# Block 0's outputs take later places in VectorE's order (eleven empty slots for six, pauses of one slot for two), and wo for block 0 is loaded from SyncE's queue

## The chip, the cores and the metric

The kernel runs on one core of one Trainium2 chip. Five engines work on their own instruction streams and meet through semaphores: TensorE (PE in the profile, with its weight loads as PEld), VectorE (DVE), ScalarE (ACT), GpSimd (POOL) and SyncE (SP), which here only starts DMAs. The metric is the device time of one execution in microseconds, taken as the median of several runs.

## The reference

One transformer block on 2048 tokens of width 512: layer norm, attention with 32 query heads of width 16 that share one key and one value head, a residual, a second layer norm, a gated feed-forward of width 1792, a second residual.

```python
q = (x @ wq).reshape(B, S, H, Dh).transpose(0, 2, 1, 3)
k = x @ wk
v = x @ wv
scores = einsum("bhqd,bkd->bhqk", q, k) * Dh ** -0.5
o = einsum("bhqk,bkd->bhqd", softmax(scores), v)
h = x + o.transpose(0, 2, 1, 3).reshape(B, S, H * Dh) @ wo
h2 = h + (gelu(ln(h) @ w_gate) * (ln(h) @ w_up)) @ w_down
```

Here x stands for the layer norm of the input in the first four lines, and for the input itself in the residual.

## The kernel before, in words

**Tiling.** The 2048 tokens are four blocks of 512. In each block the 32 heads go in 8 groups of 4, and each group runs over 16 chunks of 128 keys. A step is half a chunk: `score` makes two score matmuls (L411) into a tile `s`, and ScalarE takes the exponential (L415) into `p`. Two steps make a chunk, and `weigh` (L419) then adds its weighted values to `acc`, one PSUM bank for the whole group. The counter `n` counts the half chunks; one group is 32 of them, one block 256. A float32 product is made of three matmuls on high and low parts (`hi`, `lo`), so nearly every operand has to be split in two by VectorE or GpSimd first.

**What runs in block 0.** While block 0 is scored, TensorE also projects the queries of blocks 1 to 3 (`project_q`, tiles `pq`). These projections share TensorE's rows with the score matmuls: a score product uses 50 rows in one half of the array, a projection matmul 64 rows in the other half. There is one PSUM bank for `pq` at a time (`width = 1`). When the first half of a `pq` is done VectorE copies a column of it (`mark`, L212), and when it is whole VectorE copies it out (`pq_raw`, L227), splits it (`qh`, `ql`) and squares it (`qs`); SyncE stores the parts to DRAM (`q_d`, L253). The next `pq` can be written only when `pq_raw` has been copied.

**The outputs' way back.** After its last chunk a group's `acc` is copied out by VectorE (`evacuate`: `oT`, L432) and written by SyncE to DRAM (`acc_d`, L436). `turn_out` reads it back in another layout with four DMAs into `oc` (L445). Two groups fill one `oc`. Then VectorE inverts the softmax sums in four pieces (`invert`, L459, called the reciprocals), multiplies (`divide`, L462), and splits the product (`high`, `low`: `o_hi` L470, `o_lo` L474). The product with wo (`pp`, L610) of the block reads `o_hi` and `o_lo`.

**What sets the order.** The order on VectorE, SyncE, TensorE, ScalarE and GpSimd is that in which the code emits the instructions, and each engine runs its own in that order: an instruction that waits holds all behind it. In blocks 1 to 3 the steps of the way back go out at fixed places. In block 0 they go through the list `outs`: `evacuate` appends to it, and the loop over `n` takes one entry per slot from its front (L1117 to L1120; a slot is one step, or two or three of them where the row of MIXED mixes projections in). An empty entry takes up a slot and emits nothing. For group 1, 3 or 5 `evacuate` appends the group's `turn_out`, six empty entries, four reciprocals and `divide`, `high`, `low`, one to a slot; a `turn_out` of group 2 or 4 is appended behind what is still there. Whenever a `pq_raw` has been emitted, the list pauses for two slots (`pause`, L231). After group 7 the list is emptied at once (L504 to L506), so that for the last pair the empty entries count for nothing.

```python
for _ in range(runs):
    if outs and not pause[0] and n % (2 * KC) not in (2, 3, 4):
        take_out()
    pause[0] = max(pause[0] - 1, 0)
```

**wo and the weights.** During block 0 GpSimd splits wo, w_gate, w_up and w_down (`part_weights`): SyncE loads a raw piece (L519), GpSimd splits it (L121, L122) and stores it to DRAM from its own queue (L528, L534). When block 0 has been scored, `load_wo(0)` (L584) reads the split wo back, two transfers of 1 MB, into memory that block 0's early tiles held until then: it waits for the last user of that memory. Block 0 takes these from GpSimd's queue, the other blocks from SyncE's. The block's `pp` begins 16 steps after the end of block 0's scores, mixed into block 1's scores. A second pass (`attend(False)`) is in the program for inputs whose scores exceed a bound; it does not run here.

Of the kernel before, what the change touches and what calls it, by code (L numbers as in the profile page):

```python
# [54 lines left out]
def kernel(  # L55
# [12 lines left out]
    nc = tc.nc  # L68
# [48 lines left out]
    def split(eng_hi, hi, lo, src, eng_lo=None):  # L117
        if eng_hi is nc.scalar:
            nc.scalar.activation(hi, src, AF.Copy)
        else:  # L120
            eng_hi.tensor_copy(hi, src)  # L121
        (eng_lo or nc.vector).tensor_tensor(lo, src, hi.bitcast(F32), op=ALU.subtract)  # L122
# [37 lines left out]
    def run(outer, first):  # L160
# [10 lines left out]
        def psum1(name):  # L171
            return ps.tile([P, T], F32, tag="d", bufs=width, name=name)
# [16 lines left out]
        def project_q(b, cs, eng, col, whole=None):  # L189
# [6 lines left out]
            for c in cs:  # L196
                pq = psum1(f"pq_{b}_{c}")
                terms = [
                    (wt[:, d, c * P : (c + 1) * P], xt[:, d, :])
                    for d in range(DC)  # L200
                    for wt, xt in ((wq_hi, xT_hi), (wq_hi, xT_lo), (wq_lo, xT_hi))
                ]
                last = len(terms) - 1
                full = c in whole
                for n, (lhsT, rhs) in enumerate(terms if full else ()):
                    nc.tensor.matmul(pq, lhsT, rhs, start=(n == 0), stop=(n == last))  # L206
                    if n % 3 == 2 and (urgent or n < last):
                        yield 3
                for a in range(2) if not full else ():
                    if a:  # L210
                        mark = eb.tile([P, 1], F32, tag="qmark", bufs=2, name=f"mark_{b}_{c}")
                        nc.vector.tensor_copy(mark, pq[:, :1])  # L212
                    rows = slice(64 * a, 64 * a + 64)
                    for n, (lhsT, rhs) in enumerate(terms):
                        yield a, last - n, partial(
                            nc.tensor.matmul, pq, lhsT[rows], rhs[rows],
                            start=(a == 0 and n == 0), stop=(a == 1 and n == last),
                            skip_group_check=True,
                        )

                raw = None
                if (b, c) in HURRY or not full:
                    raw = eb.tile([P, T], F32, tag="vT", bufs=3, name=f"pq_raw_{b}_{c}")
                    if b == 0:
                        nc.scalar.activation(raw, pq, AF.Copy)
                    else:
                        nc.vector.tensor_copy(raw, pq)  # L227
                    if full:
                        yield 3
                    else:  # L230
                        pause[0] = 2  # L231
                if halves and norms:
                    yield REST
                    norms.pop()()
                qh = eb.tile([P, T], F32R, tag="qh", bufs=2, name=f"qh_{b}_{c}")
                ql = eb.tile([P, T], F32R, tag="ql", bufs=2, name=f"ql_{b}_{c}")
                if raw is not None:
                    split(nc.vector, qh, ql, raw)
                else:

                    split(nc.vector if b == 0 and c == FIRST_Q else eng, qh, ql, pq)
                qs = eb.tile([P, T], BF16, tag="qs", bufs=DC, name=f"qs_{b}_{c}")
                square = partial(
                    (nc.gpsimd if urgent else nc.vector).tensor_tensor,
                    qs, qh.bitcast(F32), qh.bitcast(F32), op=ALU.mult,
                )
                if full:
                    square()
                else:
                    squares.append(square)  # L250
                qss.append(qs)
                for r0, part in ((0, qh), (DH, ql), (2 * DH, qh)):
                    nc.sync.dma_start(  # L253
                        q_d[c * HC : (c + 1) * HC, r0 : r0 + DH, tsl].bitcast(F32),
                        part.bitcast(F32),
                    )
                if not halves and (raw is None or b == 0):
                    yield 3
# [56 lines left out]
        after, squares, norms, pause = [], [], [], [0]  # L315
# [81 lines left out]
        o_blk, pair, outs, last_out = {}, [None], [], []  # L397
# [28 lines left out]
        def take_out():  # L426
            for step in outs.pop(0):
                step()

        def evacuate(b, g, acc):  # L430
            oT = sb.tile([P, T], F32, tag="oT", bufs=2, name=f"oT_{b}_{g}")
            nc.vector.tensor_copy(oT, acc)  # L432
            c, k = divmod(g, 2)
            last = b == NB - 1 and g == NG - 1
            if not last:
                nc.sync.dma_start(acc_d[:, g % 4, :], oT)  # L436
            if k == 0:
                pair[0] = sb.tile([P, 2, T], F32, tag="oc", bufs=2, name=f"oc_{b}_{c}")
            oc = pair[0]

            def turn_out():
                view = acc_d[:, g % 4, :].rearrange("(j s e) t -> j e s t", s=2, e=DH)
                for j in range(4):
                    r0 = 64 * k + DH * j
                    nc.sync.dma_start(oc[r0 : r0 + DH, :, :], view[j])  # L445

            def gather():

                for s in (1, 0):
                    for j in range(4):  # L450
                        r0 = 64 * k + DH * j
                        (nc.sync if s or j == 0 else nc.scalar).dma_start(
                            oc[r0 : r0 + DH, s, :], oT[(2 * j + s) * DH : (2 * j + s + 1) * DH, :]
                        )


            def invert(t):
                sl = slice(t * P, (t + 1) * P)
                nc.vector.reciprocal(oc[:, 1, sl], oc[:, 1, sl])  # L459

            def divide():
                nc.vector.tensor_tensor(oc[:, 0, :], oc[:, 0, :], oc[:, 1, :], op=ALU.mult)  # L462

            def high():
                if c == 0:
                    o_blk[b] = [
                        sb.tile([P, DC, T], F32R, tag=f"o_{w}", bufs=1, name=f"o_{w}_{b}")
                        for w in ("hi", "lo")
                    ]
                nc.vector.tensor_copy(o_blk[b][0][:, c, :], oc[:, 0, :])  # L470

            def low():
                hi, lo = o_blk[b]
                nc.vector.tensor_tensor(  # L474
                    lo[:, c, :], oc[:, 0, :], hi[:, c, :].bitcast(F32), op=ALU.subtract
                )


            def piece(t):
                sl = slice(t * P, (t + 1) * P)  # L480
                hi, lo = o_blk[b]
                invert(t)
                nc.vector.tensor_tensor(
                    oc[:, 0, sl], oc[:, 0, sl], oc[:, 1, sl], op=ALU.mult
                )
                split(nc.vector, hi[:, c, sl], lo[:, c, sl], oc[:, 0, sl], nc.gpsimd)

            if b == 0 and g < NG - 1:
                outs.append([turn_out])
            elif not last:  # L490
                turn_out()
            if last:
                last_out.extend([piece, gather])
            elif k == 1:

                if b == 0:
                    outs.extend([[] for _ in range(6)])
                    outs.extend([partial(invert, t)] for t in range(TB))
                    outs.extend([step] for step in (divide, high, low))
                else:  # L500
                    outs.append([])
                    outs.extend([partial(invert, t), partial(invert, t + 1)] for t in (0, 2))
                    outs.append([divide, high, low])
            if b == 0 and g == NG - 1:  # L504
                while outs:
                    take_out()  # L506
# [73 lines left out]
        def load_wo(b):  # L580

            for j in range(DC // 2):
                w = db.tile([P, 2, 2, D], F32R, tag="w2", bufs=W2, name=f"wo_{b}_{j}")
                (nc.sync if b else nc.gpsimd).dma_start(  # L584
                    w.bitcast(F32),
                    wo_d[2 * j : 2 * j + 2].rearrange("c p i d -> p c i d").bitcast(F32),
                )
                wos[b, 2 * j], wos[b, 2 * j + 1] = w[:, 0], w[:, 1]
# [559 lines left out]
        for c in range(LEAD[0], (NB - 1) * NG * len(SIZES)):  # L1148
            b, cb = divmod(c, NG * len(SIZES))
# [398 lines left out]
```

## Time and profile before

| | before |
|---|---|
| median of 3 runs | 1420.72 us (1418.92 to 1421.18) |
| profiled execution, own time | 1415.9 us |
| span in its trace | 1414.2 us |
| granted TensorE clock, mean | 0.999 |
| TensorE busy | 1393.1 us |
| ScalarE busy | 1041.1 us |
| VectorE busy | 552.0 us |
| GpSimd busy | 185.9 us |
| moved by DMA | 193.68 MB, 137 GB/s in the mean |

The span runs from the first to the last instruction in the trace; the profiled execution's own time is 1.7 us more. In the views quoted below, a row of the waits is "engine, tile, line <- what it waited for: us in total, times, longest". A row of the order in time is "start, duration, engine, line, operation, xcount, and in brackets the idle time of that engine just before, with what ended it". A row of the chain is "start, duration, what": it is followed back from the last instruction, at each step to what released it. SPq is SyncE starting a DMA; "issue" is time in which nothing that the profile shows was waited for. Block 0's scoring with projections lies between about 75 and 285 us, the end of block 0's last group at 304 us.

### The profile page before, as it was taken

How to read it: one execution, taken by the hardware profiler on the slowest of the kernel's cores; microseconds unless marked ns; L12 is line 12 of the kernel's file. 1: busy time of each engine (PE TensorE's matmuls, PEld its weight loads, DVE VectorE, ACT ScalarE, POOL GpSimd, SP SyncE). 2: the span in 40 equal slices, each digit the busy share in tenths (PEclk: the TensorE clock that was granted, in tenths of full speed). 3: DMA queues.
4: the chain of work that ended last, by engine and by line, in shares of the span. 5: the costliest groups of instructions: out<-in, count | busy, mean ns of one | idle time of the engine just before them, and what ended most of it. 6: DMA issues, size and time to landing. Idle time of an engine off the chain costs nothing.

```text
span 1414.2 us, 25575 instructions
## 1 busy us (share of the span) xinstructions
PE 1393.1 (99%) x10622; PEld 781.9 (55%) x10622; DVE 552.0 (39%) x980; ACT 1041.1 (74%) x1149; POOL 185.9 (13%) x280
## 2 busy tenths in 40 slices
PE   8999999999999999999999999999999999999998
PEld 7533333324555555555555555554555555557886
DVE  7421432323252433434252432414352342427664
ACT  7699989996778777777788777877787777772000
POOL 6355556521000000000000000000000000002000
PEclk9999999999999999999999999999999999999999
DMA  4467887861241332223252332223243241435551
GB/s 159 160 203 250 249 251 255 249 219 52 102 157 64 117 117 87 87 85 138 87 174 72 117 117 87 87 91 116 102 143 105 87 147 45 142 124 199 184 195 57
DMA packets 84647, 193.68 MB, mean 137 GB/s; under 512 B 9684, under 2 KB 24020, under 8 KB 84492
## 3 DMA queue, kind: packets, MB, share of 16 engines
q1 hardware_dynamic: 77028, 165.41, 35.1%
q0 software_dynamic: 7328, 26.46, 5.2%
q8 instruction: 85, 1.39, 0.4%
q14 instruction: 38, 0.31, 0.1%
q10 hardware_dynamic: 168, 0.10, 0.0%
HBM read 142.12 MB, written 49.55 MB: 136 GB/s over the span
## 4 chain that ended last, share of the span: by engine, by line
PE 90%; ACT 4%; DMA 2%; DVE 1%; issue 1%; SPq 1%; POOL 0%; DVEq 0%; ACTq 0%; POOLq 0%
PE acc L419 32%; PE s L411 18%; PE pu L933 8%; PE pg L933 8%; PE pd L933 5%; ACT p L415 3%; PE pq L409 3%; PE pd L610 3%; PE pd L632 3%; PE pg L632 3%; PE pu L632 3%; PE pp L610 2%; PE pq L206 1%; DMA acc_d<-oT 1%; PE pp L741 1%
## 5 line engine op out<-in xcount | busy, mean ns | idle before, releaser
L415 ACT ACTIVATE p<-s 128x1024 f32<-128x1024 f32 x1024 | 969.7, 1034 | 230.2 <-PE s L411 226.6
L419 PE MATMUL acc<-p,v_sb 128*32 128x512 f32 x4096 | 494.1, 598 | 0.1
L411 PE MATMUL s<-qg,kaug 50*128 50x512 f32 x1984 | 417.1, 425 | 4.1 <-ACT p L415 3.9
L411 PEld LDWEIGHTS s<-qg,kaug 50*128 50x128 f32 x1984 | 193.5, 184 | 224.8 <-ACT p L415 128.6
L419 PEld LDWEIGHTS acc<-p,v_sb 128*32 128x32 f32 x4096 | 109.6, 109 | 227.4 <-issue 223.5
L933 PE MATMUL pu<-x2h,w 64*128 64x512 f32 x672 | 212.1, 391 | 0.0
L933 PE MATMUL pg<-x2h,w 64*128 64x512 f32 x672 | 211.2, 390 | 0.5 <-DVE mark_pg L956 0.5
L933 PEld LDWEIGHTS pg<-x2h,w 64*128 64x128 f32 x672 | 116.0, 185 | 14.6 <-DVE mark_pg L956 0.9
L933 PEld LDWEIGHTS pu<-x2h,w 64*128 64x128 f32 x672 | 116.1, 185 | 13.5
L933 PE MATMUL pg<-x2l,w 64*128 64x512 f32 x336 | 122.0, 391 | 0.0
L933 PE MATMUL pu<-x2l,w 64*128 64x512 f32 x336 | 122.0, 390 | 0.0
L810 ACT ACTIVATE ga<-ga 128x512 f32<-128x512 f32 x56 | 35.3, 634 | 89.2 <-DVE ga L805 89.2
L131 POOL TENSOR_SCALAR rstd<-mv 128x1 f32<-128x1 f32 x16 | 3.5, 221 | 681.6 <-DVE mv L129 681.5
L933 PE MATMUL pd<-w,gh 64*128 64x512 f32 x384 | 81.1, 392 | 0.0
L875 DVE TENSOR_TENSOR h<-h,pd 128x512 f32<-128x512 f32 x48 | 31.9, 684 | 115.4 <-PE pd L933 66.4
L459 DVE RECIPROCAL oc<-oc 128x128 f32<-128x128 f32 x64 | 56.7, 924 | 45.8 <-DMA w_0r<-in_B_w_gate_dram 21.4
L1175 DVE SCALAR_TENSOR_TENSOR ga<-ga,g 128x512 f32<-128x512 f32 x70 | 48.4, 691 | 52.7 <-ACT ga L810 51.6
L432 DVE COPY oT<-acc 128x512 f32<-128x512 f32 x32 | 22.1, 691 | 119.7 <-PE acc L419 119.5
L794 DVE COPY g<-pg 128x512 f32<-128x512 f32 x56 | 38.7, 692 | 63.4 <-PE pg L933 57.7
L933 PEld LDWEIGHTS pg<-x2l,w 64*128 64x128 f32 x336 | 58.0, 185 | 7.2
L933 PEld LDWEIGHTS pu<-x2l,w 64*128 64x128 f32 x336 | 58.1, 185 | 6.5
L807 DVE SCALAR_TENSOR_TENSOR g<-g,pu 128x512 f32<-128x512 f32 x56 | 38.3, 685 | 40.3 <-PE pu L933 30.2
(245 smaller groups left out, 1437.1 us busy)
## 6 DMA issues: line engine op xcount, KB each, us to landing
w<-w_d SPq DMA_DIRECT2D x112, 512.0 KB
w<-w_d SPq DMA_DIRECT2D x28, 1024.0 KB
qg<-q_d SPq DMA_DIRECT2D x48, 200.0 KB
q_d<-qh SPq DMA_DIRECT2D x32, 256.0 KB
acc_d<-oT SPq DMA_DIRECT2D x31, 256.0 KB
oc<-acc_d SPq DMA_DIRECT2D x124, 64.0 KB
w_d<-w_0b POOLq DMA_DIRECT2D x14, 512.0 KB, 6.9
w_d<-w_1b POOLq DMA_DIRECT2D x14, 512.0 KB, 5.8
```

The source lines that it names most:

```text
L409: step()
L411: nc.tensor.matmul(s[:, a, :], kaug[rows, kc * P : (kc + 1) * P], qg[rows, 2 * u + a, :], start=True, stop=True,)
L415: nc.scalar.activation(p[:, 2 * u : 2 * u + 2, :], s, AF.Exp, scale=SCALE)
L419: nc.tensor.matmul(acc[32 * j : 32 * j + 32, :], v_sb[:, kc, :], p[:, j, :], start=(kc == 0), stop=(kc == KC - 1), skip_group_check=True,)
L459: nc.vector.reciprocal(oc[:, 1, sl], oc[:, 1, sl])
L610: nc.tensor.matmul(banks[k], lhsT[rows], rhs[rows], start=(turn == 0 and i == 0), stop=(turn == 1 and i == n - 1), skip_group_check=True,)
L632: nc.tensor.matmul(bank, lhsT, rhs, start=(i == 0), stop=(i == len(ts) - 1))
L794: nc.vector.tensor_copy(g, pg)
L807: nc.vector.scalar_tensor_tensor(g, g, 0.5, pu, op0=ALU.mult, op1=ALU.mult)
L810: nc.scalar.activation(a, a, AF.Tanh, scale=GELU_A * GELU_C)
L933: nc.tensor.matmul(e["bank"], lhsT[rows], rhs[rows], start=i == 0 and not e["both"], stop=last and e["both"], skip_group_check=True,)
L1175: (soon or lazy).pop(0)()
```

## The change

Three edits. The list `outs` of block 0 gets eleven empty entries between a pair's `turn_out` and its first reciprocal instead of six. The pause after a `pq_raw` is one slot instead of two. And block 0's wo is loaded from SyncE's queue like that of the other blocks, not from GpSimd's.

```diff
                     if full:
                         yield 3
                     else:
-                        pause[0] = 2
+                        pause[0] = 1
...
                 if b == 0:
-                    outs.extend([[] for _ in range(6)])
+                    outs.extend([[] for _ in range(11)])
                     outs.extend([partial(invert, t)] for t in range(TB))
                     outs.extend([step] for step in (divide, high, low))
...
                 w = db.tile([P, 2, 2, D], F32R, tag="w2", bufs=W2, name=f"wo_{b}_{j}")
-                (nc.sync if b else nc.gpsimd).dma_start(
+                nc.sync.dma_start(
                     w.bitcast(F32),
```

TensorE's and ScalarE's instructions keep their order. VectorE's order changes for the pairs of groups (0, 1), (2, 3) and (4, 5). For the pair (2, 3) it stood as follows on VectorE, while the last `pq` of block 2 (`pq_3`) and the first of block 3 (`pq_0`) were made; the numbers behind the names count tiles:

```order
L212 COPY mark_3_2210<-pq_3_2109 128x1
L459 RECIPROCAL oc_1_1791<-oc_1_1791 128x128
L227 COPY pq_raw_3_2302<-pq_3_2109 128x512
L121 CAST qh_3_2304<-pq_raw_3_2302 128x512
L122 TENSOR_TENSOR ql_3_2305<-pq_raw_3_2302,qh_3_2304 128x512
L1116 TENSOR_TENSOR qs_3_2308<-qh_3_2304 128x512
L459 RECIPROCAL oc_1_1791<-oc_1_1791 128x128 x3
L212 COPY mark_0_2406<-pq_0_2312 128x1
L462 TENSOR_TENSOR oc_1_1791<-oc_1_1791 128x512
L432 COPY oT_4_2446<-acc_4_2085 128x512
L470 CAST o_hi_1856<-oc_1_1791 128x512
```

And the same place on VectorE now:

```order
L212 COPY mark_3_2210<-pq_3_2109 128x1
L227 COPY pq_raw_3_2301<-pq_3_2109 128x512
L121 CAST qh_3_2303<-pq_raw_3_2301 128x512
L122 TENSOR_TENSOR ql_3_2304<-pq_raw_3_2301,qh_3_2303 128x512
L1116 TENSOR_TENSOR qs_3_2307<-qh_3_2303 128x512
L212 COPY mark_0_2402<-pq_0_2311 128x1
L459 RECIPROCAL oc_1_1788<-oc_1_1788 128x128
L432 COPY oT_4_2442<-acc_4_2085 128x512
L459 RECIPROCAL oc_1_1788<-oc_1_1788 128x128
L227 COPY pq_raw_0_2490<-pq_0_2311 128x512
```

The first reciprocal of this pair stood ahead of a `pq_raw` and now stands behind that `pq_raw`, its splits and the next `mark`. The other two pairs move alike: the pair (0, 1) has all four reciprocals behind `oT_2` and the `mark` after it, and the pair (4, 5) has its first behind the last `mark`.

On SyncE's queue the read-backs of groups 2 and 4 (`oc`) move back, because the list is longer. The read-back of group 2 stood like this, between weight loads (`w_0r`, `w_1r`) and the stores of a query part (`q_d`):

```order
L436 DMA acc_d<-oT_2_1788 128x512
L391 DMA qg_4_1796<-q_d 50x4x512 x2
L519 DMA w_0r<-in_B_w_gate_dram 128x4x128
L519 DMA w_1r<-in_B_w_up_dram 128x4x128
L445 DMA oc_1_1791<-acc_d 16x2x512 x4
```

It now stands behind three stores and two weight loads more, ahead of the next `w_1r`; that of group 4 moves behind one weight load. Those of groups 1, 3 and 5, on which the reciprocals depend, keep their places.

The third place is the end of block 0. Before, GpSimd's queue held the two loads of wo behind the last store of a query bound (`m`):

```order
L290 TENSOR_SCALAR m_0_3202<-qn_0_3198,mm_0_3201 32x512
L294 DMA q_d<-m_0_3202 32x512
L584 DMA wo_0_3352<-wo_d 128x2x1024
L584 DMA wo_1_3354<-wo_d 128x2x1024
L131 TENSOR_SCALAR rstd_0_0_3626<-mv_0_0_3623 128x1
```

Now SyncE's queue holds them, ahead of the write of group 7's output and its read-back:

```order
L1470 DMA b_d<-q2m 32x1
L584 DMA wo_0_3352<-wo_d 128x2x1024
L584 DMA wo_1_3354<-wo_d 128x2x1024
L436 DMA acc_d<-oT_7_3383 128x512
L445 DMA oc_3_3103<-acc_d 16x2x512 x4
L391 DMA qg_1_3397<-q_d 50x2x512 x2
```

So the two loads moved from the end of GpSimd's work for block 0 to a place on SyncE between the check value `b_d` and group 7's way back; what stands behind that is as before.

## The prediction

> **What bounds the kernel now.** I read the head of the page first, then the waits of TensorE, then the chain at the place they name, then the order in time around it.
>
> ```profile
> span 1414.2 us, 25575 instructions
> PE 1393.1 (99%) x10622; PEld 781.9 (55%) x10622; DVE 552.0 (39%) x980; ACT 1041.1 (74%) x1149; POOL 185.9 (13%) x280
> PE 90%; ACT 4%; DMA 2%; DVE 1%; issue 1%; SPq 1%; POOL 0%; DVEq 0%; ACTq 0%; POOLq 0%
> ```
>
> TensorE is busy 1393.1 of 1414.2 us and holds 90% of the chain. The change adds and removes no work of TensorE, so it can gain only what TensorE waits for; 21.1 us are left in all. The waits list says for whom:
>
> ```profile
> PE pq L409 <- DVE pq_raw L227: 3.0, 1, 3.0
> PE pp L610 <- DMA w<-w_d: 0.3, 1, 0.3
> ```
>
> One wait stands out: a single one of 3.0 us, for a VectorE copy of a projection. The chain shows what held that copy:
>
> ```profile
> 182.50 8.17 DMA acc_d<-oT
> ...
> 192.03 7.20 DMA oc<-acc_d
> ...
> 199.41 0.09 DVE oc L459
> 199.50 0.78 issue
> 200.28 0.64 DVE pq_raw L227
> ...
> 200.96 0.50 PE pq L409
> ```
>
> Group 3's output needed 8.17 us to reach DRAM and 7.20 us to come back. The first reciprocal stood on VectorE ahead of `pq_raw` and waited for it to 199.41 us. In VectorE's waits that is the longer of two (the list names a weight load; the chain names `oc`, which the reciprocal reads, and I go by that):
>
> ```profile
> DVE oc L459 <- DMA w_0r<-in_B_w_gate_dram: 21.4, 2, 13.2
> ```
>
> What it cost is read on the two engines that set the pace, in order of time:
>
> ```profile
> 195.00 0.40 PE L409 MATMUL pq<-xT_hi,wq_lo 64*128 64x512 f32 x1
> 197.46 0.49 PE L411 MATMUL s<-qg,kaug 50*128 50x512 f32 x2
> 200.96 0.50 PE L409 MATMUL pq<-xT_hi,wq_hi 64*128 64x512 f32 x1 [3.01 <-DVE pq_raw L227]
> 198.00 1.02 ACT L415 ACTIVATE p<-s 128x1024 f32<-128x1024 f32 x1
> 201.80 1.94 ACT L415 ACTIVATE p<-s 128x1024 f32<-128x1024 f32 x2 [2.78 <-PE s L411]
> 203.92 1.02 ACT L415 ACTIVATE p<-s 128x1024 f32<-128x1024 f32 x1 [0.18 <-PE s L411]
> ```
>
> The `pq` was whole at 195.40 us and could have been copied then; the copy began at 200.28. TensorE stood 3.01 us, ScalarE 2.78 us.
>
> **The change part by part.**
>
> *The reciprocals of the pair (2, 3).* `pq_raw` now comes ahead of the first of them. It can start at 195.40 and ends, at 0.64 us, by about 196.1, before TensorE wants the bank at 197.95. The 3.01 us go. What is late next is ScalarE: its exponential ends at 199.02, and the next scores would be there at 198.79 (201.80 less 3.01), so it starts the first exponential 2.78 us earlier; after its two it would be done at 200.96, and the next scores come at 203.92 less 3.01 = 200.91. From there the gain is 2.96, and the 0.05 left comes back at ScalarE's next idle time, where TensorE again sets the pace. I take **3.0 us**.
>
> Whether the wait comes back at the new place: the first reciprocal now stands behind the next `mark`.
>
> ```profile
> 208.09 0.16 DVE L212 COPY mark<-pq 128x1 f32<-128x1 f32 x1 [2.13 <-PE s L411]
> 212.32 0.69 DVE L432 COPY oT<-acc 128x512 f32<-128x512 f32 x1 [2.73 <-PE acc L419]
> 215.90 0.69 DVE L227 COPY pq_raw<-pq 128x512 f32<-128x512 f32 x1 [2.55 <-PE s L411]
> 221.57 0.69 DVE L474 TENSOR_TENSOR o_lo<-oc,o_hi 128x512 fp32r<-128x512 f32 x1
> 226.15 0.16 DVE L212 COPY mark<-pq 128x1 f32<-128x1 f32 x1 [3.89 <-PE pq L409]
> ```
>
> That `mark`, 3.0 us earlier, ends at 205.3; the data was there at 199.2 and keeps its place on SyncE. The margin is 6 us, and the next work behind, the copy `oT`, is due only at 209.3: landing must slip by 10 us before TensorE feels it. One reciprocal (0.94) fits in the 2.73 us ahead of `oT` and one in the 2.55 us ahead of `pq_raw`. The tightest place is ahead of the `mark` at 226.15: two reciprocals, `divide` and `o_hi` now stand there, `o_lo` moves behind it.
>
> ```profile
> L459 DVE RECIPROCAL oc<-oc x64: 889/942/954, 136.8 to 1283.9; 128x128 f32<-128x128 f32 x64
> L462 DVE TENSOR_TENSOR oc<-oc x15: 682/692/1524, 150.8 to 1209.9; 128x512 f32<-128x512 f32 x15
> L470 DVE CAST o_hi<-oc x15: 417/426/1390, 152.3 to 1210.6; 128x512 fp32r<-128x512 f32 x15
> ```
>
> By the medians (the middle number, ns) that is 2 x 0.94 + 0.69 + 0.43 = 3.0 us; by the largest, 2 x 0.95 + 1.52 + 1.39 = 4.8. The room is 3.89 + 0.69 = 4.6 us. So it costs nothing, at worst 0.2 us.
>
> [...]
>
> *The pair (0, 1).* Here the first reciprocal waited too, 8.2 us, and delayed its `pq_raw`:
>
> ```profile
> 137.43 0.39 PE L409 MATMUL pq<-xT_hi,wq_lo 64*128 64x512 f32 x1
> 136.82 0.95 DVE L459 RECIPROCAL oc<-oc 128x128 f32<-128x128 f32 x1 [8.21 <-DMA w_0r<-in_B_w_gate_dram]
> 137.86 0.69 DVE L227 COPY pq_raw<-pq 128x512 f32<-128x512 f32 x1
> 149.70 0.16 DVE L212 COPY mark<-pq 128x1 f32<-128x1 f32 x1 [0.64 <-PE pq L409]
> 159.10 0.69 DVE L227 COPY pq_raw<-pq 128x512 f32<-128x512 f32 x1 [4.67 <-PE s L411]
> ```
>
> But that `pq` was whole only at 137.82, and the copy began at 137.86: nothing was lost, nothing is won. The four reciprocals now follow the `mark` at 149.70; with `divide` they take 4 x 0.95 + 1.52 = 5.3 us at most and are done by 155.2, ahead of the `pq_raw` at 159.10. Zero.
>
> *The pair (4, 5).* Its first two reciprocals had no idle time ahead of them:
>
> ```profile
> 259.19 1.76 DVE L459 RECIPROCAL oc<-oc 128x128 f32<-128x128 f32 x2
> ```
>
> They move to later places, behind that `mark`: zero. The shorter pause and the read-backs of groups 2 and 4 act only through this order, and no reciprocal waits for those two without also waiting for groups 3 and 5 behind them.
>
> *wo from SyncE.* It still waits for the last store of a bound, which GpSimd starts at 293.46.
>
> ```profile
> 293.46 0.57 POOL L294 DMA_DIRECT2D q_d<-m  x1 [0.29 <-POOL m L290]
> 296.25 1.49 POOL L584 DMA_DIRECT2D wo<-wo_d  x2 [2.22 <-ACT p L415]
> 304.80 0.34 SPq L436 DMA_DIRECT2D acc_d<-oT  x1
> 306.88 1.72 SPq L445 DMA_DIRECT2D oc<-acc_d  x4
> 315.40 0.43 DVE L470 CAST o_hi<-oc 128x512 fp32r<-128x512 f32 x1
> 319.78 0.63 PE L610 MATMUL pp<-wo,o_hi 64*128 64x512 f32 x4
> 298.00:303.00 5.00, 5.00 (x40) 1.49 (x36) 0.00 (x0) 5.00 (x6) 0.00 (x0) 1.00 0.97 377
> 304.00:305.00 1.00, 1.00 (x11) 0.47 (x12) 0.69 (x1) 1.00 (x3) 0.00 (x0) 1.00 0.00 0
> ```
>
> The wo transfers filled the DMA engines from 298 to 303 us (share 0.97, 377 GB/s) and were over when group 7's write was started at 304.80 (share 0.00). TensorE now arrives 3.0 us earlier, GpSimd perhaps not: group 7's write then starts at 301.8, with wo ahead of it on the same queue until about 303.5, and lands by about 305 instead of 303.9. Its cover: `o_hi` of the last pair is ready at 315.83 and first used at 319.78 (`out_terms` goes through the four pairs in order, and this is the fourth), 3.95 us later, and both move together. A delay of 1.1 us is hidden. Taken as zero; the bounds are 0.3 us gained (the wait of `pp`) and the second rival below.
>
> Sum: 1415.9 - 3.0 = 1412.9 us for the profiled execution. The median shown is 4.8 us above that execution, so 1420.7 - 3.0 = **1417.7 us**.
>
> **The rivals.**
>
> *The stall is larger in other executions.* All three timed runs are 3.0 to 5.3 us above the profiled one. If `oc` lands later there, every us goes straight to TensorE, since the copy is already 4.9 us late. With half of the 4.8 us from this wait the gain is 3.0 + 2.4 = 5.4: 1415.3 us. For it: both legs of that trip, 8.17 and 7.20 us, are waits in a full queue, against 2.06 us for the same write in an empty one (304.80 to 306.86). Against: nothing shows where the 4.8 us lie. Chance 0.15.
>
> *The gain is given back.* The wait was also a pause in which the DMA engines caught up. Now the query stores of that `pq` start about 5 us earlier, among the loads, and VectorE's sequence is fuller at the tight `mark`. If half is lost, the gain is 1.5: 1419.2 us. Against: every margin above is over 1 us except that one. Chance 0.16.
>
> *wo holds group 7's way back.* SyncE runs in order, and wo stands ahead of group 7's write; before, it stood on another queue. If GpSimd's splitting falls behind, wo starts late, and `o_hi` is late for `pp`. The point from which it decides: `o_hi` may be 3.95 us late, and 1.1 of these are used, so wo must start 2.8 us later than 296.25. To turn the 3.0 gained into 3.0 lost it must start 9 us later, at about 305: 1423.7 us. For it: GpSimd spent block 0 waiting for its loads and stores, and has nothing in hand at the end. Against: none of its work is added, and the two issues leave it. Chance 0.10.
>
> [...]
>
> *The change does not do what it says* for the last pair, whose list is emptied at once; so the way back ahead of `pp` gains nothing from eleven slots. That is in the sum.
>
> **How the numbers follow.** The forecast has 0.59. About 0.2% of the time, 2.8 us, is what a measurement of this kernel can tell from no change, and the forecast lies just beyond that bound, so I divide it: 0.32 faster by over 0.2%, 0.25 within, 0.02 slower by chance of the runs. With the larger stall (0.15) faster is 0.47; the gain given back (0.16) is within; wo (0.10) is slower. Together 0.47, 0.41, 0.12. The range goes from the larger stall with 0.8 us for the spread of the runs, 1414.5, up to no change with the same spread, 1421.5; the third rival's end is left out.
>
> **What would show it.** Right: no TensorE wait for `pq_raw` over 0.5 us, ScalarE without an idle time of 2.8 us near 199, `pq_raw` within 0.2 us of its last matmul, group 7's `oT` copy at 301 instead of 304.08, the same 3.0 us at every later stage. wo right: its loads started by SyncE at 296 or before, and the first `pp` at 314. Wrong: a reciprocal that waits for `oc` again at its new place, a `mark` that TensorE waits for, or an `acc_d` write that SyncE starts well behind its `oT`. It would also be wrong if the 3.0 us are gone at `oT` but back by the end.

## The result and the profile after

The changed kernel takes **1413.22 us**, the median of 21 runs (1411.93 to 1419.93). The kernel before, in runs alternating with these, takes 1416.47 us, the median of 21 (1413.80 to 1421.18). The ratio is 0.9977 with a 95% interval of [0.9966, 0.9988]: 3.25 us faster, and by the interval 1.7 to 4.8 us. The three runs of before that stood ahead of the prediction (median 1420.72) are among its slower ones. One more execution of before, of 1531.83 us at a mean granted clock of 0.85, counts in no number below.

The head of the page of the changed kernel and its chain by engine:

```profile
span 1410.3 us, 25577 instructions
PE 1393.8 (99%) x10622; PEld 780.3 (55%) x10622; DVE 551.3 (39%) x980; ACT 1040.9 (74%) x1149; POOL 184.6 (13%) x278
PE 92%; ACT 4%; DMA 2%; DVE 1%; issue 1%; POOL 0%; SPq 0%; DVEq 0%; ACTq 0%; POOLq 0%
```

TensorE's work is the same (1393.8 against 1393.1 us); the span is 3.9 us shorter, and TensorE's idle time is shorter by 4.6 us (21.1 against 16.5). In TensorE's waits the row of 3.0 us for `pq_raw` is gone, and no row of its size has come in:

```profile
PE s L411 <- ACT p L415: 4.4, 15, 0.7
```

VectorE, TensorE and ScalarE in order of time, around the place where the wait was and around the tight `mark`:

```profile
195.48 0.69 DVE L227 COPY pq_raw<-pq 128x512 f32<-128x512 f32 x1 [9.21 <-PE s L411]
...
204.89 0.16 DVE L212 COPY mark<-pq 128x1 f32<-128x1 f32 x1 [6.50 <-PE s L411]
205.54 0.95 DVE L459 RECIPROCAL oc<-oc 128x128 f32<-128x128 f32 x1 [0.49 <-DMA q_d<-ql]
...
217.16 1.11 DVE L122 TENSOR_TENSOR ql<-pq_raw,qh 128x512 fp32r<-128x512 f32 x1
218.20 1.77 DVE L1116 TENSOR_TENSOR qs<-qh 128x512 bf16<-128x512 f32 x1
219.89 1.75 DVE L459 RECIPROCAL oc<-oc 128x128 f32<-128x128 f32 x2
221.68 0.69 DVE L462 TENSOR_TENSOR oc<-oc 128x512 f32<-128x512 f32 x1
222.40 0.43 DVE L470 CAST o_hi<-oc 128x512 fp32r<-128x512 f32 x1
222.96 0.16 DVE L212 COPY mark<-pq 128x1 f32<-128x1 f32 x1
```

```profile
222.53 0.39 PE L409 MATMUL pq<-xT_hi,wq_lo 64*128 64x512 f32 x1
```

```profile
176.23 30.20 ACT L415 ACTIVATE p<-s 128x1024 f32<-128x1024 f32 x32 [0.18 <-PE s L411]
```

`pq_raw` is copied at 195.48 (200.28 before), the first reciprocal stands behind the next `mark` at 205.54, and ScalarE runs 32 exponentials without a pause across the place where it stood 2.78 us. At the tight place the matmul that `mark` waits for ends at 222.92 and `mark` starts at 222.96, as close behind it as before (226.11 and 226.15). `o_hi` ended at 222.83, so VectorE came in time by 0.09 us; TensorE has no wait for it.

The end of block 0 did not go as forecast. GpSimd's and SyncE's rows, and the chain there:

```profile
297.69 0.57 POOL L294 DMA_DIRECT2D q_d<-m  x1 [0.29 <-POOL m L290]
```

```profile
299.90 0.90 SPq L584 DMA_DIRECT2D wo<-wo_d  x2
301.59 0.34 SPq L436 DMA_DIRECT2D acc_d<-oT  x1
308.47 1.73 SPq L445 DMA_DIRECT2D oc<-acc_d  x4
```

```profile
301.59 6.87 DMA acc_d<-oT
...
316.29 0.44 DVE o_hi L470
...
316.77 0.73 PE pp L610 x2
```

TensorE was 3.2 us earlier there (`oT` is copied at 300.87, not 304.08), but GpSimd's last store came 4.2 us later than before (297.69 against 293.46). So wo started at 299.90, the DMA engines were full of it (share 0.88 to 1.03 in each stretch of 2 us from 302 to 308), and group 7's write took 6.87 us instead of 2.06. In the chain `o_hi` ended at 316.73 (316.29 and 0.44), and TensorE used it from 316.77: of the cover of 3.95 us, 0.04 us were left. In the profiled execution this cost nothing.

### The profile page after: what moved, and what is told of

Same layout as the page of the kernel before. It is cut to its first block, busy times and chain, and to the rows that moved or that the text cites. A ratio compares the mean times of both kernels' runs of the same rounds, so it can differ in the third digit from the quotient of the medians.

```text
span 1410.3 us, 25577 instructions
## 1 busy us (share of the span) xinstructions
PE 1393.8 (99%) x10622; PEld 780.3 (55%) x10622; DVE 551.3 (39%) x980; ACT 1040.9 (74%) x1149; POOL 184.6 (13%) x278
## 4 chain that ended last, share of the span: by engine, by line
PE 92%; ACT 4%; DMA 2%; DVE 1%; issue 1%; POOL 0%; SPq 0%; DVEq 0%; ACTq 0%; POOLq 0%
PE acc L419 32%; PE s L411 18%; PE pu L933 9%; PE pg L933 8%; PE pd L933 5%; PE pq L409 3%; ACT p L415 3%; PE pd L610 3%; PE pd L632 3%; PE pg L632 3%; PE pu L632 3%; PE pp L610 2%; PE pq L206 1%; DMA x<-in_A_x_dram 1%; PE pp L741 1%; DMA acc_d<-oT 1%
```

## The experiments

In all kernels below the whole computation is done. Each median stands beside the median of the kernel before from the same chip.

**One edit each.** Four kernels, edits to the kernel before: the eleven entries alone, the pause alone, wo's queue alone, and the first two together.

```diff
-                    outs.extend([[] for _ in range(6)])       # e1, e4
+                    outs.extend([[] for _ in range(11)])
-                        pause[0] = 2                          # e2, e4
+                        pause[0] = 1
-                (nc.sync if b else nc.gpsimd).dma_start(      # e3
+                nc.sync.dma_start(
```

> Only the eleven slots; the pause stays at two slots and wo on GpSimd's queue. First theory (the gain is the reciprocal of the pair (2, 3) that no longer stands ahead of pq_raw): TensorE's 3.0 us wait for pq_raw is gone, about 3 us less than before, group 7's oT copy at about 301. Rival (the gain comes from wo's queue, or from the shorter pause): no gain, within 0.5 us of before.

> Only the shorter pause; six slots, wo on GpSimd's queue. The first reciprocal of the pair (2, 3) still stands ahead of the same pq_raw. First theory: TensorE still waits about 3 us for pq_raw, within 0.5 us of before. Rival (the shorter pause carries the gain): 3 us less and no such wait.

> Only wo from SyncE's queue; six slots, pause of two. First theory: the 3 us wait stays and nothing is gained, since wo has 4 us of cover; group 7's write lands at most 2 us later than before and pp does not wait; within 0.5 us of before. Rival (the queue of wo carries the gain): 3 us less.

> The whole change but for wo, which stays on GpSimd's queue. First theory: the same gain as the whole change, about 3 us, and group 7's write no longer stands behind wo on one queue: it lands in 2 to 4 us where the whole change took 6.87, so o_hi of the last pair is ready 3 to 4 us ahead of its use instead of 0.04 us. Rival (wo's queue is part of the gain): less than 2 us gained.

| kernel | median us (runs) | ratio to before | wait for `pq_raw`, profiled |
|---|---|---|---|
| before | 1417.15 (34) | | |
| e1, eleven entries | 1414.14 (12) | 0.9979 [0.9967, 0.9991] | none |
| e2, pause | 1417.65 (12) | 1.0000 [0.9987, 1.0013] | 3.3 us |
| e3, wo on SyncE | 1416.29 (12) | 0.9995 [0.9979, 1.0010] | 1.7 us |
| e4, both of outs | 1414.20 (12) | 0.9981 [0.9971, 0.9991] | none |

The eleven entries alone give the gain; the pause adds nothing to them, and neither the pause nor wo's queue gives anything measurable by itself. The runs also show what slows group 7's write. In e1 and e4 wo is on GpSimd's queue. The chain and GpSimd's row of e1:

```profile
301.90 7.27 DMA acc_d<-oT
```

```profile
300.13 1.49 POOL L584 DMA_DIRECT2D wo<-wo_d  x2 [2.22 <-PE s L411]
```

And those of e4:

```profile
301.36 2.06 DMA acc_d<-oT
```

```profile
293.91 1.49 POOL L584 DMA_DIRECT2D wo<-wo_d  x2 [2.23 <-PE s L411]
```

With wo started at 300.13 the write takes 7.27 us though it is on another queue, as long as behind wo on its own queue (6.87 in the changed kernel); with wo started at 293.91 it takes 2.06. When wo starts decides, and that follows GpSimd's last store, which came between 286.90 (e3) and 299.97 us (e5, below). In e5 wo started only at 302.77: the write took 2.05 us, and it was the read-back that took 8.17. In both kernels with wo late on GpSimd's queue, the cover was used up and TensorE waited, in e1 and in e5:

```profile
PE pp L610 <- DVE o_hi L470: 0.3, 1, 0.3
```

```profile
PE pp L610 <- DVE o_hi L470: 0.6, 1, 0.6
```

Five of the six profiles without the wait for `pq_raw` have GpSimd's last store at 297.34 or later (e4 is the other, 291.12); all seven with it, e8 left out, have it at 295.01 or before. That would fit the rival by which the wait let the DMA engines catch up, but no run tries it, and why GpSimd ends so differently stays open.

**One pair alone, and back.** e5 is the kernel before with eleven entries for the pair (2, 3) only; e6 is the changed kernel with six for that pair only.

```diff
-                    outs.extend([[] for _ in range(6)])                      # e5
+                    outs.extend([[] for _ in range(11 if c == 1 else 6)])
...
-                    outs.extend([[] for _ in range(11)])                     # e6
+                    outs.extend([[] for _ in range(6 if c == 1 else 11)])
```

> Before, with eleven slots for the pair (2, 3) alone; the other two pairs keep six, the pause stays at two and wo on GpSimd's queue. Theory (one reciprocal ahead of one pq_raw is the whole gain): the TensorE wait for pq_raw is gone and the gain is that of the whole change, about 3 us. Rival (part of the gain lies with the other pairs, the pause or wo): clearly less, 1.5 us or under.

> The whole change, with six slots for the pair (2, 3) alone, so that its first reciprocal stands ahead of pq_raw again. Theory: the wait of TensorE for pq_raw is back, 2 to 3.5 us, and the time is that of before within 0.7 us. Rival: over half of the gain stays, 1.5 us or more faster than before.

e5 took 1413.75 us (8 runs), ratio 0.9967 [0.9955, 0.9980]; e6 took 1417.27 us (12 runs), ratio 0.9991 [0.9977, 1.0005]; before 1418.04 (19). One pair's place gives the whole gain, and with that pair put back nothing measurable is left (e6's interval reaches from 3.3 us faster to 0.7 slower, so the wait that is back says more than its time). e6's wait and the granted clock from there on (in the windows: TensorE, weight load, VectorE, ScalarE and GpSimd busy, then the granted clock, DMA share and GB/s):

```profile
PE pq L409 <- DVE pq_raw L227: 3.6, 1, 3.6
```

```profile
200.00:202.00 2.00, 0.53 (x2) 0.50 (x4) 1.93 (x4) 0.00 (x0) 0.41 (x1) 0.50 1.06 348
202.00:204.00 2.00, 2.00 (x12) 0.87 (x12) 2.00 (x2) 1.21 (x2) 1.91 (x2) 0.50 0.72 224
204.00:206.00 2.00, 2.00 (x12) 0.57 (x6) 2.00 (x3) 0.73 (x1) 1.61 (x4) 0.50 0.54 178
```

This was not in my account: the clock fell to half during the wait, at about 200.0 us (0.99 in the 2 us before), and came back only at about 206.8 (0.80 from 206 to 208; the wait ended at 201.47), so the wait costs more than its own length. In e2 and e3 it fell behind the wait (0.70 from 202 to 204 us and 0.75 from 200 to 202, 1.00 in the 2 us before).

**wo twice.** In the changed kernel each wo load is issued twice from SyncE, into the same memory, to try the price of the second rival.

```diff
-                nc.sync.dma_start(
+                for _ in range(1 if b else 2):
+                    nc.sync.dma_start(
...
```

> The whole change, with each of the two loads of wo issued twice from SyncE's queue (the second overwrites the first with the same values), so 2 MB more stand ahead of group 7's write. In the profile of the whole change o_hi of the last pair was ready 0.04 us ahead of its use, so the cover of 3.95 us was used up. Theory (wo ahead of group 7's write has a price once that cover is gone): the write lands about 5 to 8 us later, pp waits for o_hi by that less what cover is left, and the kernel loses 3 to 8 us against the whole change, 0 to 5 us against before. Rival (DMA engines take the write between wo's packets, or the read-back has more cover than worked out): no wait of pp over 1 us, the gain of 3 us stays.

It took 1425.72 us (4 runs), ratio to before 1.0057 [1.0037, 1.0078]. Its waits, and SyncE's rows (line numbers are one higher):

```profile
PE pp L611 <- DVE o_hi L470: 7.0, 1, 7.0
...
PE pp L611 <- DMA wo<-wo_d: 4.2, 2, 3.9
```

```profile
300.29 14.29 SPq L585 DMA_DIRECT2D wo<-wo_d  x4
314.68 0.41 SPq L436 DMA_DIRECT2D acc_d<-oT  x1
```

SyncE stood 14.29 us in the four issues (0.90 for two in the changed kernel), presumably because a second load into the same memory waited for the first, so the write was issued 13 us later than in the changed kernel and TensorE waited 7.0 us for `o_hi` and 3.9 for wo. The rival's mechanism is real; e1 and e5 show its beginning, just beyond the cover. The loss is larger than expected: wo itself was late as well, and the clock stood at 0.50 from about 319.2 to 332.8 us (0.96, 0.50 and 0.86 in the three stretches of 10 us from 310 on).

**No weight pieces around group 3's trip.** In the kernel before, the weights' pieces are left out of the half chunks 113 to 139 and go two at a time in 140 to 179.

```diff
-                    next(parts, None)
+                    for _ in range(0 if 112 < n < 140 else 2 if 140 <= n < 180 else 1):
+                        next(parts, None)
```

> Before, with no weight pieces started while group 3 ends (n from 113 to 139) and two at a time after it (140 to 179), so that no weight loads stand in the queue ahead of group 3's read-back; the first reciprocal stays ahead of pq_raw. Theory (the length of the wait is the trip of oc through a full queue): the trip from the start of the write to the first reciprocal falls from 16.9 us to under 12, oc is there when pq is whole, and the 3 us wait shrinks to under 0.5 us, unless the loads that are late take it back elsewhere. Rival (the trip is slow for another reason than the weight loads): the write and the read-back stay at 7 to 8 us each and the wait at 2 us or more.

It took 1427.62 us (6 runs), ratio 1.0067 [1.0052, 1.0082]. The waits of TensorE and the chain at group 3's write:

```profile
PE pq L409 <- DVE mark L212: 10.9, 1, 10.9
...
PE pq L409 <- DVE pq_raw L227: 0.5, 1, 0.5
```

```profile
181.23 8.55 DMA acc_d<-oT
```

The wait for `pq_raw` fell to 0.5 us, in part because that write was issued 1.3 us earlier than before (181.23 against 182.50); the write still took 8.55 us (8.17 before), and from its start to the first reciprocal it was 16.2 us (16.9 before), not under 12. SyncE started no weight load between 164.46 and 191.61 us, so the loads are not what makes the write slow. What does is open: query stores and score loads are in those queues too, and GpSimd started the store of one piece at 179.61, 1.6 us ahead of the write. The time was lost later, where the postponed pieces stood on SyncE ahead of group 5's write and read-back, and a reciprocal ahead of a `mark`:

```profile
261.99 0.37 SPq L519 DMA_DIRECT2D w_1r<-in_B_w_up_dram  x1
262.41 1.23 SPq L436 DMA_DIRECT2D acc_d<-oT  x1
...
270.13 2.27 SPq L445 DMA_DIRECT2D oc<-acc_d  x4
```

```profile
276.92 1.76 DVE L459 RECIPROCAL oc<-oc 128x128 f32<-128x128 f32 x2 [20.26 <-DMA oc<-acc_d]
278.60 0.10 DVE L212 COPY mark<-pq 128x1 f32<-128x1 f32 x1
```

It is the same fault as that of the pair (2, 3), made larger: a reciprocal that waits for its trip, with a copy behind it that TensorE needs.

**wo behind group 7's way back.** In the changed kernel `load_wo(0)` moves behind group 7's read-back on SyncE.

```diff
                     db = late.enter_context(tc.tile_pool(name="dense", bufs=1))
-                    load_wo(0)
...
                 if n == 2 * PER + 8:
+                    load_wo(0)
                     primed = dense(0)
```

> The changed kernel with wo for block 0 loaded behind group 7's read-back on SyncE's queue, not ahead of its write. Theory (wo in the DMA engines' queues is what slows group 7's write, and o_hi is hidden up to the first pp anyway): the write lands about 2.1 us after its start (6.87 us with wo ahead), the last o_hi comes near 311 to 312 us (316.29), TensorE starts the first pp at 313.9 as before unless wo itself lands later than that, and the time stays at 1413 to 1414 us. Rival (wo was late enough to cost TensorE something in the executions that the profile did not catch): 1411 to 1412 us. If wo lands after 313.9, a wait of pp for wo of up to 1.5 us.

It took 1414.37 us (12 runs), ratio 0.9977 [0.9965, 0.9988]; before 1417.43 (17). The chain, TensorE's wait, and the windows behind it (the profiled execution, 1416.33 us, is the slowest of the twelve):

```profile
301.43 2.05 DMA acc_d<-oT
```

```profile
PE pp L610 <- DMA xb<-in_A_x_dram: 2.4, 1, 2.4
```

```profile
316.00:318.00 2.00, 2.00 (x12) 1.81 (x12) 0.00 (x0) 0.00 (x0) 0.00 (x0) 0.50 1.04 418
318.00:320.00 2.00, 2.00 (x16) 1.83 (x14) 0.00 (x0) 0.92 (x1) 0.00 (x0) 0.65 1.03 412
```

The write lands in 2.05 us, as expected, but now wo is late: `pp` waits 2.4 us (the list names `xb`, which this product does not read; wo stands just ahead of it on the queue, so I put the wait down to wo), with half clock behind it. The same ratio as the changed kernel: no gain. The rival of a hidden cost of wo is not refuted by it, since this edit takes one wait away and brings another; the 0.3 and 0.6 us of e1 and e5 show that such a cost occurs.

**The kernel before, three more profiles.** No edit; the question is whether the wait and the clock change from execution to execution.

> The kernel before, unchanged, in another execution with a profile. Theory (the wait for pq_raw varies from execution to execution and may be followed by a few us at half of TensorE's granted clock): a wait of 1.5 to 4 us; if the granted clock falls to 0.50 behind it, the span is 1.5 to 3 us longer than the 1414.2 us of the first profile, if it stays at 1.00, the span is within 1 us of it. Rival (the clock falls only in the edited kernels, for a reason of their own): clock 1.00 from 195 to 210 us.

> The kernel before once more, as the run e10_before, for a second look at the same question: wait of 1.5 to 4 us for pq_raw, and a span that is 1.5 to 3 us longer where the granted clock falls to 0.50 behind the wait than where it does not.

> The kernel before, a third look. Three profiles of it had waits for pq_raw of 3.0, 1.4 and 2.8 us and a granted clock of 1.00 behind them; three edited kernels with the same wait (1.7, 3.3, 3.6 us) had 0.50 behind it. Theory (the same wait is followed by half clock in some executions, whatever the kernel; about 3 in 6 so far): an even chance of 0.50 between 199 and 207 us, and then a span of 1415 to 1418 us. Rival (only the edited kernels do it): clock 1.00 and a span of 1413 to 1415 us. One look that stays at 1.00 does not decide between them.

The waits for `pq_raw` in the three, in this order:

```profile
PE pq L409 <- DVE pq_raw L227: 1.4, 1, 1.4
```

```profile
PE pq L409 <- DVE pq_raw L227: 2.8, 1, 2.8
```

```profile
PE pq L409 <- DVE pq_raw L227: 4.6, 1, 4.6
```

The windows of the third just behind the wait (it ends at 202.41), and its matmuls there:

```profile
202.00:204.00 2.00, 1.59 (x8) 1.03 (x8) 1.93 (x4) 0.41 (x1) 1.36 (x2) 0.65 0.82 283
204.00:206.00 2.00, 2.00 (x10) 0.20 (x8) 2.00 (x2) 1.53 (x2) 1.70 (x3) 0.50 0.56 163
```

```profile
202.41 0.65 PE L409 MATMUL pq<-xT_hi,wq_hi 64*128 64x512 f32 x1 [4.59 <-DVE pq_raw L227]
...
202.86 0.62 PE L409 MATMUL pq<-xT_lo,wq_hi 64*128 64x512 f32 x1
...
206.67 0.39 PE L409 MATMUL pq<-xT_hi,wq_hi 64*128 64x512 f32 x1
```

The unedited kernel does it too: a matmul takes 0.62 us behind the wait and 0.39 at 206.67. The rival that only edited kernels do it falls. The table has all profiles with the reciprocal ahead of that `pq_raw` (e8, which loses time elsewhere, left out). What TensorE has lost is read at the start of group 7's `oT` copy: in the six profiles without the wait (the changed kernel, e1, e4, e5, e7, e9) it comes at 300.64 to 301.18 us, 300.80 in the mean.

| profile | wait us | clock behind it | `oT` of group 7 at | over 300.80 | over that and the wait |
|---|---|---|---|---|---|
| e10 | 1.43 | 1.00 | 302.35 | 1.55 | 0.12 |
| e11 | 2.79 | 1.00 | 303.85 | 3.05 | 0.26 |
| before | 3.01 | 1.00 | 304.08 | 3.28 | 0.27 |
| e3 | 1.71 | to 0.50 | 304.28 | 3.48 | 1.77 |
| e2 | 3.29 | to 0.50 | 305.99 | 5.19 | 1.90 |
| e6 | 3.64 | to 0.50 | 306.98 | 6.18 | 2.54 |
| e12 | 4.59 | to 0.50 | 307.09 | 6.29 | 1.70 |

The wait is 1.4 to 4.6 us, 2.9 in the mean. The last column is 0.2 us in the mean without the clock's fall and 2.0 with it. So the one reciprocal costs 1.5 to 6.3 us, depending on the execution.

## Why the prediction was wrong, and where it was right

The cause was right and so was its size: 3.0 us forecast, 3.25 measured. The time was wrong: 1413.22 us lies 4.5 us below the forecast and 1.3 below the low end of the range.

**The step that failed** is the last of the sum: "The median shown is 4.8 us above that execution, so 1420.7 - 3.0 = 1417.7 us." It treats the 4.8 us as a constant that belongs to every run of either kernel. It was none. The median of before over 21 runs is 1416.47, 0.6 us above the profiled execution's 1415.9; the three runs shown were a sample from its upper part. In the changed kernel the median lies 1.1 us above its profiled execution. Without that step the sum stands: 1412.9 for the profiled execution, against 1412.15 measured. So of the 4.5 us, 3.7 come from this step and 0.8 from the sum.

**The first rival** ("the stall is larger in other executions", 0.15) had a mechanism that is there. The wait varies (1.4 to 4.6 us), as it said. It missed the clock, and it started from 1420.7 too, so that its 1415.3 is also too high; the low end of the range came from it and inherits the fault. "Nothing shows where the 4.8 us lie" was true of the one trace at hand. The timed runs fit this: of 70 of the kernel before, those with a mean granted clock of 0.999 (17) have a median of 1415.05, of 0.998 (28) 1417.26, of 0.997 (19) 1419.40; of the 53 runs of the kernels in whose profile the wait is gone (the changed kernel, e1, e4, e5) 39 are at 0.999 or above. They do not prove it. A mean of 0.998 can come without a fall behind the wait: e10 has it, with a clock of 1.00 from 198 to 204 us. In the first profile of before the clock fell only behind the last matmul (which ends at 1407.43): 1.00 up to 1408 us, 0.92 from there to 1412, 0.50 from 1412 to 1414. And two runs of the changed kernel took 1419.19 and 1419.93 us. That the slow timed runs arise at this place is inferred: they have no trace.

**Step by step.** *The pair (2, 3):* right. `pq_raw` starts 0.03 us behind its last matmul (195.45); e5 and e6 show that this pair is the gain. *The reciprocal at its new place:* right, it does not hold the `mark`. *The tight `mark`:* right that it costs nothing, but 0.09 us were left where the medians left 1.6. I let only `divide` and `o_hi` grow, and these took 0.69 and 0.43; what grew were `ql` and `qs` ahead of them, 1.11 and 1.77 us where before had 0.69 each. They ran beside GpSimd's split of a weight piece (217.12 to 219.41), which was over before them in the kernel before (at 218.64, `ql` from 220.36). That the two slowed each other is my estimate from this place; no run tries it. *Pairs (0, 1) and (4, 5), and the pause:* right, zero (e2; e6 keeps both new places and gains nothing measurable). *wo from SyncE:* zero, but by luck of 0.04 us. I let group 7's write land 1.1 us late; it took 4.8 us longer than in before (6.87 against 2.06). "Its loads started by SyncE at 296 or before" was wrong (299.90). The mis-sized term is GpSimd's end, which I took from one execution (293.46) and which lies between 286.90 and 299.97 in the runs; in the four profiles of the unedited kernel it moves by 1.8 us only. *One queue or two for wo and the write:* no run shows a difference; the write took 6.87 us behind wo on one queue (the changed kernel) and 7.27 us beside it on another (e1). *The gain given back* and *wo holds group 7's way back:* neither happened in the changed kernel's profile. The second is nearer than my 2.8 us said: in e1 and e5, with wo on GpSimd's queue, `pp` waited 0.3 and 0.6 us for `o_hi`.

## What to carry to other kernels

In a list that mixes work from a DMA with work that the pacing engine waits for, the place of one instruction decides: put what waits for a trip behind the copy that frees the pacing engine's buffer, with a margin for the trip's spread and not its one profiled length. Anchor a forecast on many runs, or on the profiled execution alone; the gap between one profile and three runs is no constant to carry over, and a wait that varies is itself a likely cause of it. A cover read from one trace is worth what the slowest of its parts does in other traces.

## What was not expected of the hardware

The granted clock fell to 0.50 in or just behind single waits of TensorE of 1.7 (e3), 2.4 (e9), 3.3 (e2), 3.6 (e6) and 4.6 us (e12), but stayed at 1.00 behind waits of 1.4 (e10), 2.8 (e11) and 3.0 us (before). What decides it no run shows: the wait of 1.71 us had the fall, the one of 3.01 us did not. By the mean clock of the stretches of 10 us around it, the time at 0.50 was 3.4 us in e2, e3, e9 and e12 (0.83), 6.8 in e6 (0.66) and, summed over three and two such stretches, 13.6 in e7 and e8. By estimate 3.4 us at half clock lose half of that, 1.7 us; the table of the seven profiles shows 1.70 to 1.90 over the wait in the three with that length (e2, e3, e12), and 0.12 to 0.27 in the three without a fall. e3's wait and windows:

```profile
PE pq L409 <- DVE pq_raw L227: 1.7, 1, 1.7
```

```profile
198.00:200.00 2.00, 0.38 (x4) 0.34 (x6) 1.90 (x3) 0.98 (x1) 0.07 (x1) 1.00 0.99 356
200.00:202.00 2.00, 2.00 (x16) 0.50 (x12) 1.97 (x3) 1.55 (x2) 1.92 (x2) 0.75 0.76 257
202.00:204.00 2.00, 2.00 (x12) 1.17 (x8) 2.00 (x3) 0.66 (x2) 0.97 (x3) 0.50 0.55 188
```

And a write of 256 KB landed in 2.06 us where the DMA engines' share had been 0.00 just ahead of it (before, 304 to 305 us), and in 6.87 us (the changed kernel) and 7.27 us (e1) right behind the start of wo's 2 MB, on the same queue there and on another here (one profile for each).
